# New durations in a planner's table, a margin for attention on TensorE, and later weight sums

## The chip, the cores and the metric

The kernel runs on one core of one Trainium2 chip. The metric is the device time of the whole program in microseconds (us). TensorE is called PE here, its weight loads PEld, VectorE DVE, ScalarE ACT, GpSimd POOL and the queue that issues the DMAs SP.

## The reference, cut to what matters

Everything is fp32. Attention with a sliding window of 64 keys over 4 batches, 8 heads, 576 positions and 64 values a head feeds two feed-forward layers with 2304 tokens:

```
scores = scale * q @ k.T ; masked to 0 <= i - j < 64 ; attn = softmax(scores)
x  = attn @ v                               # (2304, 512)
x  = softplus(x @ w_in) @ w_out             # d_ff 2048, first layer
y  = (sigmoid(x @ w_gate) * (x @ w_val)) @ w_out2   # d_ff 1536, second layer
```

## The kernel before, in words

**Products.** fp32 values are split into a high and a low part, and each product is three matmuls (`mm3`, lines 358 to 360). The weights arrive as fp64 in 512 KB pieces of 128x512 numbers. ACT scales one half of the bits (`w_scale`, line 114), DVE does three bit operations (`w_shift` 119, `w_sign` 123, `w_low` 128), ACT makes the high part (`w_hi`, 134) and POOL the low one (`w_lo`, 139). The 32 pieces of the first layer stay in SBUF.

**First layer.** Tokens go in five blocks (`BLOCKS1`: 512, 384, 384, 512, 512). A slot is one group of 12 matmuls: `m1_proj(b, f)` (h from x and w1) or `m1_out(b, f)` (adds into four accumulators acc). Block b has 16 of each, alternating, so block 0 is slots 0 to 33, and block 1 begins at slot 30. Piece i of the weights is first needed by slot i. Between the two stand `m1_act` (softplus on ACT, 377), `g_hi` (ACT, 384) and `g_lo` (POOL, 390). h has two PSUM buffers, so a projection waits for the softplus of two projections earlier.

**Attention.** 36 groups of 64 queries; the first 8 (`NG0`, "early") come before block 0, the others are done while the block before theirs is in the slots. One group is: `att_scores` (PE, 256), `att_max` (DVE, 268 and 271), `att_exp` (ACT, 283; for later groups in pairs, with a table load before and one after, at the next softplus), `att_sum` (DVE, 288 and 289), `att_norm` (POOL, 294), a transpose (PE 302 in block 0; from groups of block 2 on through DVE 310 and two DMAs, `pd` and `pt`, 316 and 323), `att_values` (PE, 340), `att_hi` (ACT, 348), `att_lo` (DVE, 353, writes xt). Scores, transposes and values share two PSUM buffers named at: values wait until `att_max` or `att_lo` has emptied one.

**Second layer.** Three stages of 768 tokens by a scheme with seven products (x2 blocks and weight sums). The weight sums (here: combos) are made during the first layer, one for each of 12 f: `c_load` of two pieces, scale and bit operations as above, `c_sums` (DVE, 153 to 155), `c_sum4` (160), `c_hi` (ACT, 178), `c_lo` (POOL, 182) and four `c_send` DMAs (187) back to HBM. `wc_load` reads them in the second layer.

**The order.** Every step is given a slot and a rank by hand (`at`). Combo f stands at slot `COMBO0 + int(COMBO * f)`. For all that lies before the second layer (`t < end`, slot 158 or so), `lead_in` then simulates the engines: among the next `AHEAD` steps by rank it takes the one that can start soonest (ties within `SLACK` by rank), with the duration that `traits` gives for it, and emits the instructions in that order. Each engine then runs its own instructions strictly in that order and waits by semaphores. So a duration in the table changes no instruction, only where it stands in its engine's queue. A DMA has in `traits` an issue time and a latency.

Of the kernel before, what the change touches and what calls it, by code (L numbers as in the profile page):

```python
# [19 lines left out]
BLOCKS1 = [512, 384, 384, 512, 512]  # L20
HALF = 384
LAG = 2
LEAD = 7
COMBO0, COMBO = 36, 9.8
WO0, WO = 6, 10
FAR = 2
RG = 0.9
SLACK = 0.15
AHEAD = 160
STB, PB, VB, GB, RB, BB = 3, 2, 2, 3, 3, 3  # L30

# [2 lines left out]
def tile_kernel(ctx: ExitStack, tc: tile.TileContext, qk, vt, w1, w2, wg, wv, wo, out):  # L34
# [21 lines left out]
    w1, w2, wg, wv, wo = (w.bitcast(U32) for w in (w1, w2, wg, wv, wo))  # L56
# [141 lines left out]
    NG0 = BLOCKS1[0] // Q  # L198
# [331 lines left out]
    for c in range(total2):  # L530
        prods = [(m2_prod, *divmod(c, NF2), k) for k in range(7)]
        outs = [(m2_out, *divmod(c - 1, NF2), i) for i in range(NCH)] if c else tail
        for entry in "M0 M1 o0 o1 M2 M3 o2 M4 M5 o3 o4 M6 o5".split():
            kind, k = (prods, outs)[entry[0] == "o"], int(entry[1])
# [158 lines left out]
    index = {key: i for i, (key, _) in enumerate(allw)}  # L693
    groups = range(NT // Q)

    def turned(g):
        return (att_blocks if grp_block[g][0] >= FAR else att_transpose, g)

    def traits(fn, a, *rest):
        early = fn.__name__.startswith(("att", "v_")) and a < NG0  # L700
        f = rest[-1] if rest else a
        if fn in (w_load, c_load):
            freed = (w_low, a) if fn is w_load else (c_send, (a - NSLOT) // 2, "av"[a % 2])
            f = (a - NSLOT) // 2 - 1
            deps = [(w_load, NSLOT - 1)] if f == -1 else [(c_hi, f, "x")] if f >= 0 else []
# [5 lines left out]
        if fn is att_scores:  # L711
            if early:
                deps = [(k_load, a // 2), (q_load, a)] + [(k_load, a // 2 - 1)] * (a % 2 == 0 and a > 0)
                return "pe", 0.55, 0, deps, [(f"s{a % 2}", 1, (att_max, a))]
            return "pe", 0.45, 0, [(qk_load, a), turned(a - 2)], [("at", 2, (att_max, a))]
        if fn is att_max:
            return "dve", 1.4, 0, [(att_scores, a)], [] if early else [("p", PB, turned(a))]
        if fn is att_exp:
            if early:
                return "act", 1.65, 0, [(att_max, a)], []  # L720
            return "act", 7.2, 0, [(att_max, a - 1), (att_max, a)], []
        if fn is att_sum:
            return "dve", 0.35, 0, [(att_exp, exp_of(a))], []
        if fn is att_norm:
            return "pool", 1.05, 0, [(att_sum, a)], []
        if fn is att_transpose:
            return "pe", 0.5, 0, [(att_norm, a)], [(f"t{a % 2}", 1, (att_copy, a)) if early else
                                                   ("at", 2, (att_copy, a))]
# [6 lines left out]
        if fn is att_copy:  # L735
            return "act", 0.6, 0, [(att_transpose, a)], [("pt", 2, (att_values, a))]
        if fn is att_values:
            return "pe", 0.5, 0, [(att_copy, a), (att_fetch, a), (v_load, a)], [("at", 2, (att_lo, a))]
        if fn is att_hi:
            b, off = grp_block[a]  # L740
            return "act", 0.4, 0, [(att_values, a)], [("xt", 2, (m1_proj, b, NF1 - 1))] * (off == 0)
# [2 lines left out]
        if fn is w_scale:  # L744
            kind, f = allw[a][0]
# [1 line left out]
            order = [(w_scale, NSLOT - 1) if a < NSLOT + 2 else (c_sums, (a - NSLOT) // 2 - 1)] * (a >= NSLOT)  # L747
            return "act", 0.67, 0, [(w_load, a), (c_load, a)] + order, [("bits", BB, freed)]
        if fn is w_shift:
            return "dve", 0.5, 0, [(w_scale, a)], []  # L750
        if fn in (w_sign, w_low):
            return "dve", 0.85, 0, [(w_shift if fn is w_sign else w_sign, a)], []
        if fn is w_hi:
            deps = [(w_low, a)]
            if a < NSLOT:
                deps += [(att_values, g) for g in range(NG0)] * (a >= NSLOT - 2 * NG0)
            else:
                kind, f = seq1[place[a]][0]
                deps.append((m1_proj if kind == "w1" else m1_out, NB1 - 1, f))
            return "act", 0.62, 0, deps, []  # L760
        if fn is w_lo:
            return "pool", 1.4, 0, [(w_hi, a)], []
        if fn is c_sums:
            return "dve", 1.3, 0, [(w_low, index["wg", a]), (w_low, index["wv", a])], [("bits", BB, (c_lo, a, "x"))]
        if fn is c_sum4:
            return "dve", 0.45, 0, [(c_sums, a), (c_lo, a, "a")], []
        if fn is c_hi:
            dep = {"a": (w_low, index["wg", a]), "s4": (c_sum4, a)}.get(f, (c_sums, a))
            return "act", 0.62 if f != "s4" else 0.4, 0, [dep], [("raw", RB, (c_send, a, "x"))] * (f == "x")
        if fn is c_lo:  # L770
            return "pool", 1.3 if f != "s4" else 0.75, 0, [(c_hi, a, f)], []
        if fn is c_send:
            return "sp", 1.0, 2.0, [(c_lo, a, f)], []
        if fn is m1_proj:
            deps = [(w_lo, index["w1", f])] + [(att_lo, g) for g in groups if grp_block[g][0] == a]
            deps += [slots[pos[fn, a, f] - 1]] * (a + f > 0)
            return "pe", 12 * (BLOCKS1[a] / 2400 + 0.0137), 0, deps, [(f"h{f % 2}", 1, (m1_act, a, f))]
        if fn is m1_act:
            return "act", 0.56, 0, [(m1_proj, a, f)], [("tb", 2, (g_lo, a, f))]
        if fn is g_hi:  # L780
            return "act", 0.56, 0, [(m1_act, a, f)], [("g", GB, (m1_out, a, f))]
        if fn is g_lo:
            return "pool", 1.25, 0, [(g_hi, a, f)], []
        if fn is m1_out:
            deps = [(g_lo, a, f), (w_lo, index["w2", f]), slots[pos[fn, a, f] - 1]]
            deps += [(m1_copy, a - 1, c) for c in range(KC)] * (f == 0)
# [8 lines left out]
            return "sp", 1.2, 2.0, [(swap_pools, 0)] + [(m1_send, b, c) for b in range(2) for c in range(KC)], []  # L795
        if fn is x2_sum:
            deps = [(x2_load, 0, x) for x in ("b11", "b12", "b22", "b21")]
            return "dve", 0.55, 0, deps + [(x2_sum, 0, k, f) for k in range(rest[0])], []
        if fn is x2_hi:
            kind, wf = seq1[2 * rest[0] + f][0]  # L800
            deps = [(x2_sum, 0, k, f) for k in range(4)] + [(m1_proj if kind == "w1" else m1_out, NB1 - 1, wf)]
            return "act", 0.5, 0, deps, []
        if fn is x2_lo:
            return "pool" if f else "dve", 1.05 if f else 0.5, 0, [(x2_hi, a, *rest)], []
        if fn is swap_pools:
            return "none", 0, 0, [(att_lo, g) for g in groups if g >= NG0], []

# [1 line left out]
    def lead_in():  # L809
        nodes = {}  # L810
        for t in sorted(events):
            if t < end:
                for order, n, fn, args in sorted(events.pop(t), key=lambda e: e[:2]):
                    nodes[fn, *args] = (t + order / 1000, *traits(fn, *args))
        free, seen, d_engine, order, rings = defaultdict(float), {}, {}, [], defaultdict(list)
        todo = sorted(nodes, key=lambda k: nodes[k][0])
        deps_of = {k: [d for d in nodes[k][4] if d in nodes] for k in todo}
        while todo:
            ready = []
            for n, key in enumerate(todo[:AHEAD]):  # L820
                rank, engine, us, lat, _, taken = nodes[key]
                deps = list(deps_of[key])
                for name, bufs, _ in taken:
                    if len(rings[name]) >= bufs:
                        deps.append(rings[name][-bufs])
                if all(d in seen for d in deps):
                    start = max([free[engine]] + [seen[d][engine != d_engine[d]] for d in deps])
                    ready.append((start, rank, n, key))
            soonest = min(r[0] for r in ready)
            start, _, n, key = min((r for r in ready if r[0] < soonest + SLACK), key=lambda r: r[1:])  # L830
            rank, engine, us, lat, _, taken = nodes[key]
            for name, _, freed in taken:
                rings[name].append(freed)
            free[engine] = start + us
            seen[key], d_engine[key] = (start + us, start + us + lat + 0.2), engine
            order.append((start, len(order), key))
            del todo[n]
        return [key for _, _, key in sorted(order)]

    with tc.manual_schedule():  # L840
        nc.scalar.preload_act_table_set("exp_and_others")
        late["apool"] = apool_cm.__enter__()
        consts()
        for fn, *args in lead_in():
            fn(*args)
        for i in sorted(events):
            for _, _, fn, args in sorted(events[i], key=lambda e: e[:2]):
                fn(*args)
# [50 lines left out]
```

## Time and profile before

| | us |
|---|---|
| median of three timed runs | 927.37 (925.10 to 928.02) |
| the profiled execution | 923.96 |
| its span, first to last instruction | 922.2 |

The mean granted TensorE clock is 0.989 of full speed. A timeline row has the start, the duration, engine, line and operation, and in brackets how long the engine was idle before it and what released it. "x16" at its end counts merged instructions. First-layer blocks lie at about 39 to 153 us (block 0), 146 to 226 (1), 226 to 311 (2), 311 to 402 (3) and 402 to 495 (4); the second layer follows.

### The profile page before, as it was taken

To read this page: it belongs to the slowest core of one execution; us is meant where nothing else is said; L and a number is where in the kernel's file an instruction comes from. 1 tells how busy PE (TensorE), PEld (TensorE's weight loads), DVE (VectorE), ACT (ScalarE), POOL (GpSimd) and SP (SyncE) were. 2 spreads that over 40 slices of the span, in tenths; PEclk is the share of its full clock that TensorE was granted. 3 is DMA by queue.
4 is the path that set the end of the run, shared out by engine and by line. 5 is a ranking of instruction groups with operands and counts; after the bars stand their busy time and mean duration, and the time that the engine had idled before them with its cause. 6 is when DMAs were issued, how large, how long until landed. Compare 5 with 4: busy or idle time off the path is not lost.

```text
span 922.2 us, 13713 instructions
## 1 busy us (share of the span) xinstructions
PE 892.3 (97%) x5024; PEld 804.5 (87%) x5024; DVE 509.2 (55%) x842; ACT 406.6 (44%) x930; POOL 358.7 (39%) x312
## 2 busy tenths in 40 slices
PE   7799898999989999999999999999999999999998
PEld 7687688999989988888888999998999998999996
DVE  4899997335343645437801667656445446444443
ACT  5787666563755665634522333324222224222222
POOL 2485676342642544445831233325111115111111
PEclk9799999999999999999999999999999999999999
DMA  8546654666666675676404676545564445544441
GB/s 310 188 162 207 208 166 159 220 216 226 216 209 214 226 263 160 200 275 235 159 1 149 228 274 228 205 160 194 194 228 160 160 160 194 195 160 160 160 160 69
DMA packets 56643, 176.54 MB, mean 191 GB/s; under 512 B 6144, under 2 KB 21248, under 8 KB 51968
## 3 DMA queue, kind: packets, MB, share of 16 engines
q1 hardware_dynamic: 56576, 175.66, 54.7%
q8 instruction: 40, 0.66, 0.3%
q14 instruction: 27, 0.22, 0.1%
HBM read 138.67 MB, written 36.96 MB: 190 GB/s over the span
## 4 chain that ended last, share of the span: by engine, by line
PE 79%; DVE 8%; ACT 5%; DMA 4%; issue 3%; POOL 1%; SPq 1%; ACTq 0%; DVEq 0%; POOLq 0%
PE h L358 14%; PE h L359 14%; PE h L360 14%; PE acc L358 9%; PE acc L359 9%; PE acc L360 9%; DMA pd<-pd 2%; DVE bits L123 2%; PE at L256 2%; DVE bits L119 2%; PE at L360 2%; PE at L359 2%; PE at L358 2%; PE acc L256 1%; DVE bits L128 1%
## 5 line engine op out<-in xcount | busy, mean ns | idle before, releaser
L466 DVE TENSOR_TENSOR t<-h,t 128x384 f32<-128x384 f32 x216 | 117.0, 555 | 198.7 <-PE h L360 190.9
L472 POOL TENSOR_TENSOR g<-t,g 128x384 fp32r<-128x384 f32 x72 | 74.9, 1040 | 288.5 <-ACT g L471 278.3
L359 PE MATMUL h<-xc,wc 128*128 128x384 f32 x504 | 169.7, 337 | 0.0
L358 PE MATMUL h<-xc,wc 128*128 128x384 f32 x504 | 169.0, 335 | 0.6 <-DVE t L466 0.4
L360 PE MATMUL h<-xc,wc 128*128 128x384 f32 x504 | 169.2, 336 | 0.0
L390 POOL TENSOR_TENSOR g<-tb,g 128x512 fp32r<-128x512 f32 (+1 forms) x80 | 101.5, 1270 | 139.4 <-ACT g L384 104.2
L358 PE MATMUL h<-xt,w 128*128 128x512 f32 (+1 forms) x320 | 120.4, 376 | 1.2 <-ACT tb L377 1.2
L358 PE MATMUL acc<-g,w 128*128 128x512 f32 (+1 forms) x320 | 121.2, 379 | 0.0
L359 PE MATMUL h<-xt,w 128*128 128x512 f32 (+1 forms) x320 | 118.8, 371 | 0.0
L360 PE MATMUL h<-xt,w 128*128 128x512 f32 (+1 forms) x320 | 118.8, 371 | 0.0
L360 PE MATMUL acc<-g,w 128*128 128x512 f32 (+1 forms) x320 | 118.3, 370 | 0.0
L359 PE MATMUL acc<-g,w 128*128 128x512 f32 (+1 forms) x320 | 118.2, 369 | 0.0
L471 ACT CAST g<-t 128x384 fp32r<-128x384 f32 x72 | 37.0, 513 | 154.8 <-DVE t L466 137.8
L358 PEld LDWEIGHTS h<-xc,wc 128*128 128x128 f32 x504 | 94.6, 188 | 9.0 <-ACT t L478 1.0
L359 PEld LDWEIGHTS h<-xc,wc 128*128 128x128 f32 x504 | 94.5, 188 | 6.5
L360 PEld LDWEIGHTS h<-xc,wc 128*128 128x128 f32 x504 | 94.7, 188 | 0.0
L139 POOL TENSOR_TENSOR w<-bits,w 128x512 fp32r<-128x512 f32 x44 | 63.8, 1450 | 54.4 <-ACT w L134 42.7
L377 ACT ACTIVATE tb<-h 128x512 f32<-128x512 f32 (+1 forms) x80 | 44.1, 551 | 89.0 <-PE h L360 88.8
L128 DVE SCALAR_TENSOR_TENSOR bits<-raw,bits 128x512 uint32<-128x512 uint32 x68 | 73.1, 1075 | 1.8
L358 PEld LDWEIGHTS h<-xt,w 128*128 128x128 f32 x320 | 61.0, 190 | 9.4 <-ACT tb L377 1.5
L358 PEld LDWEIGHTS acc<-g,w 128*128 128x128 f32 x320 | 60.6, 189 | 8.3 <-ACT x L408 0.4
L360 PEld LDWEIGHTS h<-xt,w 128*128 128x128 f32 x320 | 60.8, 190 | 7.9
(93 smaller groups left out, 1542.4 us busy)
## 6 DMA issues: line engine op xcount, KB each, us to landing
wc<-wcd SPq DMA_DIRECT2D x36, 1792.0 KB, 7.3
raw<-in_w SPq DMA_DIRECT2D x32, 512.0 KB, 3.6
qk<-in_qk SPq DMA_DIRECT2D x28, 512.0 KB, 4.8
wcd<-raw SPq DMA_DIRECT2D x24, 512.0 KB, 4.6
v<-in_vt SPq DMA_DIRECT2D x25, 256.0 KB, 4.7
raw<-in_wg SPq DMA_DIRECT2D x12, 512.0 KB, 4.6
raw<-in_wv SPq DMA_DIRECT2D x12, 512.0 KB, 4.5
wcd<-sumr SPq DMA_DIRECT2D x12, 512.0 KB, 5.3
```

The source lines that it names most:

```text
L119: nc.vector.tensor_scalar(out=t, in0=t, scalar1=3, scalar2=None, op0=ALU.logical_shift_left)
L128: nc.vector.scalar_tensor_tensor(out=t, in0=r[:, :, 0], scalar=29, in1=t, op0=ALU.logical_shift_right, op1=ALU.bitwise_or)
L139: nc.gpsimd.tensor_tensor(out=w[:, 1, :], in0=t, in1=w[:, 0, :].bitcast(F32), op=ALU.subtract)
L256: nc.tensor.matmul(out=s[:, j, at0:at0 + n], lhsT=t[:, 0, j, :], rhs=keys[:, j, :n], start=True, stop=True)
L358: nc.tensor.matmul(out=o, lhsT=lh, rhs=rh, start=first, stop=False)
L359: nc.tensor.matmul(out=o, lhsT=lh, rhs=rl, start=False, stop=False)
L360: nc.tensor.matmul(out=o, lhsT=ll, rhs=rh, start=False, stop=last)
L377: nc.scalar.activation(out=t, in_=h_t.pop((b, f)), func=AF.Softplus)
L390: nc.gpsimd.tensor_tensor(out=g[:, 1, :n], in0=t, in1=g[:, 0, :n].bitcast(F32), op=ALU.subtract)
L466: nc.vector.tensor_tensor(out=out, in0=a, in1=b, op=op)
L471: nc.scalar.copy(out=g[:, 0, :HALF], in_=t)
L472: nc.gpsimd.tensor_tensor(out=g[:, 1, :HALF], in0=t, in1=g[:, 0, :HALF].bitcast(F32), op=ALU.subtract)
```

## The change

It changes numbers only: where the combos stand, the durations in `traits`, and a margin in `lead_in`. `ROOM` is added to the time at which a step's inputs are there, for PE steps other than `m1_proj` and `m1_out` whose group is not one of the first 8. No instruction is added or removed. Where only a number changes, the old and the new one are shown with an arrow.

```diff
-COMBO0, COMBO = 36, 9.8
+COMBO0, COMBO = 52, 8.4
+ROOM = 0.5
 att_scores:
-            return "pe", 0.45, 0, [(qk_load, a), turned(a - 2)], [("at", 2, (att_max, a))]
+            return "pe", 0.9, 0, [(qk_load, a), turned(a - 2)], [("at", 2, (att_max, a))]
 att_exp (a pair):
-            return "act", 7.2, 0, [(att_max, a - 1), (att_max, a)], []
+            return "act", 5.9, 0, [(att_max, a - 1), (att_max, a)], []
 att_norm:       "pool", 1.05 -> 1.09        att_values:  "pe", 0.5 -> 0.62
 w_shift:
-            return "dve", 0.5, 0, [(w_scale, a)], []
+            return "dve", 0.74, 0, [(w_scale, a)], []
 w_sign, w_low:
-            return "dve", 0.85, 0, [(w_shift if fn is w_sign else w_sign, a)], []
+            return "dve", 0.9 if fn is w_sign else 1.15, 0, [(w_shift if fn is w_sign else w_sign, a)], []
 w_lo:           "pool", 1.4 -> 1.49         c_sums:      "dve", 1.3 -> 1.7
 c_sum4:         "dve", 0.45 -> 0.55         c_lo:        "pool", 1.3 -> 1.37 (s4 stays 0.75)
 m1_act:
-            return "act", 0.56, 0, [(m1_proj, a, f)], [("tb", 2, (g_lo, a, f))]
+            return "act", BLOCKS1[a] / 1000 + 0.09, 0, [(m1_proj, a, f)], [("tb", 2, (g_lo, a, f))]
 g_hi:           "act", 0.56 -> BLOCKS1[a] / 1000 + 0.11
 g_lo:           "pool", 1.25 -> BLOCKS1[a] * 0.0028
 x2_sum:         "dve", 0.55 -> 1.2          x2_lo:       "pool" 1.05 -> 1.37, "dve" 0.5 -> 1.1
 lead_in:
-                    start = max([free[engine]] + [seen[d][engine != d_engine[d]] for d in deps])
+                    room = ROOM if engine == "pe" and key[0] not in (m1_proj, m1_out) and key[1] >= NG0 else 0
+                    start = max([free[engine]] + [seen[d][engine != d_engine[d]] + room for d in deps])
```

## Rows read from the trace of the kernel before

**Rows 1.** Page: span, then busy time of each engine (share, instructions).

```profile
span 922.2 us, 13713 instructions
PE 892.3 (97%) x5024; PEld 804.5 (87%) x5024; DVE 509.2 (55%) x842; ACT 406.6 (44%) x930; POOL 358.7 (39%) x312
```

**Rows 2.** Windows: length, each engine's busy us (instructions), granted clock, DMA share, GB/s.

```profile
0.00:100.00 100.00, 87.32 (x558) 74.86 (x559) 83.08 (x120) 69.88 (x183) 58.24 (x52) 0.93 0.63 213
100.00:200.00 100.00, 94.20 (x601) 85.04 (x600) 68.22 (x104) 66.25 (x156) 55.99 (x47) 0.98 0.57 184
200.00:300.00 100.00, 93.76 (x650) 91.85 (x649) 41.09 (x85) 55.04 (x140) 40.52 (x40) 0.98 0.69 225
...
400.00:500.00 100.00, 100.00 (x443) 82.86 (x444) 45.52 (x53) 38.99 (x74) 52.05 (x38) 1.00 0.45 162
...
110.00:120.00 10.00, 10.00 (x44) 8.05 (x40) 8.63 (x16) 9.89 (x26) 4.69 (x4) 0.83 0.67 233
270.00:280.00 10.00, 9.81 (x63) 9.78 (x64) 2.53 (x5) 2.20 (x5) 5.39 (x6) 0.83 0.69 215
```

**Rows 3.** Waits of PE, 0 to 310 us: total us, times, longest.

```profile
PE at L340 <- DVE xt L353: 8.5, 6, 3.2
PE at L340 <- DVE p L268: 5.3, 2, 3.4
...
PE at L256 <- DVE xt L353: 2.4, 1, 2.4
PE at L340 <- DMA pt<-pd: 2.1, 3, 1.2
PE h L358 <- ACT tb L377: 1.2, 1, 1.2
```

**Rows 4.** Timeline of PE: the two waits for `att_max` in block 0.

```profile
79.82 0.68 PE L340 MATMUL at<-pt,v 64*64 64x64 f32 x16 [1.94 <-DVE p L268]
...
109.52 0.69 PE L340 MATMUL at<-pt,v 128*64 128x64 f32 x16 [3.40 <-DVE p L268]
```

**Rows 5.** Groups on DVE by form, 40 to 150 us: busy us, mean ns.

```profile
L128 DVE SCALAR_TENSOR_TENSOR bits<-raw,bits 128x512 uint32<-128x512 uint32 x30 | 39.7, 1323 | 0.9
L123 DVE SCALAR_TENSOR_TENSOR bits<-raw,bits 128x512 uint32<-128x512 uint32 x30 | 28.6, 953 | 1.0
L119 DVE TENSOR_SCALAR bits<-bits 128x512 uint32<-128x512 uint32 x29 | 23.9, 825 | 2.8 <-ACT bits L114 2.8
```

**Rows 6.** Timeline of DVE ahead of the longest wait.

```profile
106.04 0.41 DVE L119 TENSOR_SCALAR bits<-bits 128x512 uint32<-128x512 uint32 x1
...
107.22 1.65 DVE L128 SCALAR_TENSOR_TENSOR bits<-raw,bits 128x512 uint32<-128x512 uint32 x1
108.79 0.68 DVE L268 SCALAR_TENSOR_TENSOR p<-at,mask 128x512 f32<-128x512 f32 x1
```

**Rows 7.** Timeline: pieces 16 and 28 finished on POOL, their slots begun on PE.

```profile
91.05 1.47 POOL L139 TENSOR_TENSOR w<-bits,w 128x512 fp32r<-128x512 f32 x1
133.79 1.49 POOL L139 TENSOR_TENSOR w<-bits,w 128x512 fp32r<-128x512 f32 x1 [1.28 <-ACT w L134]
...
92.72 0.48 PE L358 MATMUL h<-xt,w 128*128 128x512 f32 x1
136.82 0.39 PE L358 MATMUL h<-xt,w 128*128 128x512 f32 x1
```

**Rows 8.** Timeline of ACT around a pair of exponentials in block 2.

```profile
226.26 0.66 ACT L114 ACTIVATE bits<-raw 128x512 f32<-128x512 f32 x1 [4.45 <-DMA raw<-in_wv]
227.87 1.28 ACT L283 ACT_TABLE_LOAD   x1
232.37 1.28 ACT L377 ACT_TABLE_LOAD   x1
```

**Rows 9.** Combos: line 155, one for each (ns min/median/max, first and last start).

```profile
L155 DVE TENSOR_TENSOR bits<-bits x12: 411/418/419, 150.8 to 452.4; 128x256 f32<-128x256 f32 x12
```

**Rows 10.** Group of line 114 over the span: its idle time and who ended it.

```profile
L114 ACT ACTIVATE bits<-raw 128x512 f32<-128x512 f32 x68 | 45.5, 670 | 41.1 <-DMA raw<-in_wv 22.6 <-DMA raw<-in_wg 11.8 <-DMA raw<-in_wo 3.0
```

More of the change, by code (lines that the diff above doesn't have):

```diff
@@ L724, in traits @@
         if fn is att_norm:
-            return "pool", 1.05, 0, [(att_sum, a)], []
+            return "pool", 1.09, 0, [(att_sum, a)], []
         if fn is att_transpose:
@@ L737, in traits @@
         if fn is att_values:
-            return "pe", 0.5, 0, [(att_copy, a), (att_fetch, a), (v_load, a)], [("at", 2, (att_lo, a))]
+            return "pe", 0.62, 0, [(att_copy, a), (att_fetch, a), (v_load, a)], [("at", 2, (att_lo, a))]
         if fn is att_hi:
@@ L761, in traits @@
         if fn is w_lo:
-            return "pool", 1.4, 0, [(w_hi, a)], []
+            return "pool", 1.49, 0, [(w_hi, a)], []
         if fn is c_sums:
-            return "dve", 1.3, 0, [(w_low, index["wg", a]), (w_low, index["wv", a])], [("bits", BB, (c_lo, a, "x"))]
+            return "dve", 1.7, 0, [(w_low, index["wg", a]), (w_low, index["wv", a])], [("bits", BB, (c_lo, a, "x"))]
         if fn is c_sum4:
-            return "dve", 0.45, 0, [(c_sums, a), (c_lo, a, "a")], []
+            return "dve", 0.55, 0, [(c_sums, a), (c_lo, a, "a")], []
         if fn is c_hi:
@@ L770, in traits @@
         if fn is c_lo:
-            return "pool", 1.3 if f != "s4" else 0.75, 0, [(c_hi, a, f)], []
+            return "pool", 1.37 if f != "s4" else 0.75, 0, [(c_hi, a, f)], []
         if fn is c_send:
@@ L778, in traits @@
         if fn is m1_act:
-            return "act", 0.56, 0, [(m1_proj, a, f)], [("tb", 2, (g_lo, a, f))]
+            return "act", BLOCKS1[a] / 1000 + 0.09, 0, [(m1_proj, a, f)], [("tb", 2, (g_lo, a, f))]
         if fn is g_hi:
-            return "act", 0.56, 0, [(m1_act, a, f)], [("g", GB, (m1_out, a, f))]
+            return "act", BLOCKS1[a] / 1000 + 0.11, 0, [(m1_act, a, f)], [("g", GB, (m1_out, a, f))]
         if fn is g_lo:
-            return "pool", 1.25, 0, [(g_hi, a, f)], []
+            return "pool", BLOCKS1[a] * 0.0028, 0, [(g_hi, a, f)], []
         if fn is m1_out:
@@ L797, in traits @@
             deps = [(x2_load, 0, x) for x in ("b11", "b12", "b22", "b21")]
-            return "dve", 0.55, 0, deps + [(x2_sum, 0, k, f) for k in range(rest[0])], []
+            return "dve", 1.2, 0, deps + [(x2_sum, 0, k, f) for k in range(rest[0])], []
         if fn is x2_hi:
@@ L803, in traits @@
         if fn is x2_lo:
-            return "pool" if f else "dve", 1.05 if f else 0.5, 0, [(x2_hi, a, *rest)], []
+            return "pool" if f else "dve", 1.37 if f else 1.1, 0, [(x2_hi, a, *rest)], []
         if fn is swap_pools:
```

## The prediction, on record before the change was built

> **What bounds the kernel now.** I read the page's line of busy times first, then the windows, then PE's waits, and then the timeline of the engines around each wait. PE is busy for 892.3 of 922.2 us [rows 1], so at most 29.9 us are idle, and everything else that reordering could give back is time at the lower clock. The windows [rows 2] say where: from 400 to 500 us PE is busy for all of 100.00 us, while the first three windows lose 12.7, 5.8 and 6.2 us. The change acts on the first layer and on what leads into the second; the second layer's own order is written by hand and stays. So the question is what happens to the waits before 311 us.
>
> Those are few [rows 3]. Early attention (before 39 us) waits for xt: of the 8.5 us in that row one wait of 3.2 us belongs to block 2, and 5.3 us are early. Block 0 has 5.3 us for `att_max` (p, line 268) and 2.4 us for xt at scores, 7.7 us together. Blocks 1 and 2 have 3.2 us for xt, 2.1 us for the DMA'd pt, and 1.2 us for a softplus, 6.5 us together. Two of the waits cost more than themselves. In the windows from 110 and from 270 us the granted clock is 0.83 [rows 2]: PE had stood idle for 3.40 us just before the first [rows 4] and for 3.2 us around 270, and then ran part of the window at 1.2 instead of 2.4 GHz. A mean of 0.83 over 10 us is 1.7 us of work lost, each time. Block 0 thus offers 7.7 + 1.7 = 9.4 us, blocks 1 and 2 offer 6.5 + 1.7 = 8.2 us, the early part 5.3 us.
>
> **Why block 0 waits.** The reader is to compare the table with the trace. The planner gave the three bit operations 0.5 + 0.85 + 0.85 = 2.2 us a piece; between 40 and 150 us they took 0.825 + 0.953 + 1.323 = 3.10 us [rows 5]. Over 30 pieces DVE falls 27 us behind its plan, as far as the semaphores let it. The rows ahead of the longest wait show it [rows 6]: `att_max` starts at 108.79, right behind the bit operations of line 128, and PE, whose order has values next, stands until 109.52. Planned honestly, either `att_max` comes earlier on DVE or values later on PE.
>
> The same rows show why the planner can't win all of it. One and the same operation takes 0.41 us in one place and 0.825 us in the mean of block 0 [rows 5, 6] (line 119), and DVE is filled with these operations, which feed PE too. Piece 16 leaves POOL at 91.05 + 1.47 = 92.52 us and its slot begins at 92.72, with 0.2 us to spare; piece 28 leaves at 135.28 and its slot begins at 136.82, with 1.5 us to spare [rows 7]. If PE doesn't stand at 77 and at 106 us, the slots come sooner and the pieces don't.
>
> **The change part by part**, against the profiled execution's 923.96 us (922.2 us of span and 1.8 us around it).
>
> *Durations of the bit operations, `w_lo`, `c_sums` and the other DVE and POOL rows.* The new table gives 0.74 + 0.9 + 1.15 = 2.79 us a piece, 0.31 us short of block 0's 3.10 [rows 5], so the lag falls from 27 to 9 us over 30 pieces. I expect the waits for `att_max` and xt to shrink. What is late next are the pieces: with their times unchanged, PE can come forward by 0.2 us before slot 16, by 1.5 us before slot 28 [rows 7], and by 1.5 + 2.4 = 3.9 us once the third wait has gone too. Bounds: 0 gained (every attention step drawn ahead on DVE pushes the pieces back by its own 0.68 us and more) and 9.4 us. I take 3.0 us, near the cap of 3.9 that the rows give, less one `att_max` of 0.68 us [rows 6] put ahead of a piece.
>
> *`ROOM`, and the longer scores and values.* Affected are the PE steps of 28 groups. A wait that stays in the same place shrinks by up to 0.5 us. The three pt waits sum to 2.1 us with a longest of 1.2 [rows 3]; taking the other two as 0.9 together, they lose 0.5 + 0.7 = 1.2 us. The xt wait of 3.2 us loses 0.5. The softplus wait is a projection's and gets no margin. Behind a postponed attention step its group's ACT and DVE steps come later; PE has slots to run meanwhile, and if at some point it hasn't, the cost is 0.5 us for that step. Together 1.7 us gained, between 0 and the 8.2 us of blocks 1 and 2.
>
> *`att_exp` from 7.2 to 5.9 us.* From the table load at 227.87 to the end of the next table load at 232.37 + 1.28 = 233.65 ACT is held for 5.8 us of which 1.28 us are the second load [rows 8]. So 5.9 us is right for the pair with both loads, and the old 7.2 was 1.4 us too long. What stood behind the exponentials was planned late and is now planned up to 1.3 us sooner. Cost nothing, hidden by `ROOM` for 0.5 us of it; if that cover fails, 0.8 us for a pair. Bounds -0.8 and +0.8 us for a pair, and I take 0.
>
> *`m1_act`, `g_hi`, `g_lo`, x2.* A few hundredths up or down in the first two, and x2 steps that run after 400 us, where PE is busy without a gap [rows 2]. Nothing; if that cover is gone, one x2 step of 1.2 us.
>
> *Combos later.* Combo 0 moves from slot 36 to 52, combo 11 from 143 to 144. Each moves 2 scales on ACT, 6 bit operations and 4 sums on DVE, 4 `c_hi` and 4 `c_lo`, and on SP 2 loads and 4 sends. Until now line 155 ran from 150.8 to 452.4 us [rows 9], close to the slots written down, so I expect the first one some 40 us later and the last where it was. Block 1 then has two combos in place of three, block 2 three as before, block 3 four in place of three. What a combo costs is seen on ACT, not on DVE: its scale stands at the head of ACT's queue until the load has landed, 22.6 + 11.8 = 34.4 us over 24 scales, 1.4 us each [rows 10], and whatever ACT should do next waits too. The softplus wait of 1.2 us is such a case: a scale held ACT for 4.45 us until 226.26, and the exponentials followed [rows 8]. On SP the sends now pass loads of q, k and v of other groups. Last comes the end: the last combo's slot moves by one, and it stands 43 us ahead of the second layer (452.4 against 495). Bounds: 1.2 us gained, or one more wait like block 2's of 3.2 us with its 1.7 us at the lower clock. Nearest is the row of no change, since block 2 keeps its three; I take 0.
>
> *Early part.* `ROOM` leaves it out, and only the order on DVE can move. Bounds: 5.3 us gained, or 3.1 us lost, if a whole piece of bit operations [rows 5] comes ahead of the last `att_lo`. I take 0.
>
> Sum: 3.0 + 1.7 = 4.7 us gained. 923.96 - 4.7 = 919.3 us. The profiled execution lay 3.4 us below the median of the timed runs, 927.37; on that, 922.7 us.
>
> **A page's rule against the trace.** Line 119 takes 0.41 us in one place and 0.825 us on average in block 0, where POOL works beside it [rows 5, 6]. The Trainium skill's page "SBUF — State Buffer" ("SBUF: two separate sides") says that DVE instructions with two SBUF inputs or in a two-port mode and GpSimd instructions share one pair of ports under an exclusive lock, held for the whole instruction. The trace agrees in kind. By that rule DVE and POOL are one resource in block 0, the pieces could come no sooner in any order, and the block would give 0 of its 9.4 us; that is the first rival below.
>
> **The rivals.**
> 1. *The pieces take over.* The waits for `att_max` go and waits for `w_lo` at slots 12 to 28 come in their place: block 0 gives the 0.2 us of slot 16 and, the idle time being cut into smaller pieces, half of its 1.7 us of clock; later blocks give some 0.5. 0.2 + 0.8 + 0.5 = 1.5, so 925.9 us. For it: 0.2 us of slack [rows 7]. Against: 2.4 us of block 0's waits lie behind slot 28. The page named above would have it so.
> 2. *Slower: ACT blocks at worse places in blocks 2 and 3.* The new order lets scales of combos wait for their loads just ahead of a pair of exponentials. One of block 2's three combos now ends in 3.2 + 1.7 = 4.9 us; if two of the seven combos of blocks 2 and 3 more do so, that is +9.8 us, less the 4.7 us above: 927.4 + 5.1 = 932.5 us. It decides where a scale's wait and the 5.8 us of a pair [rows 8] together exceed the time until PE needs the next h or at buffer. For it: block 2's slots are the short ones, and DMA shares there are 0.69 [rows 2]. Against: block 3's slots are a third longer, and its attention waited for next to nothing.
> 3. *Everything settles.* All waits for attention go, block 0 gives its 3.9 us and 1.7 us of clock, and blocks 1 and 2 give 6.4 of their 8.2 us: 12.0 us, so 915.4 us. For it: the table's largest error, DVE's, is mostly mended. Against: the DMA steps' issue times in the table stay as they were.
> 4. *The change doesn't do what it says:* combos follow data and not slots, and come as early as before. That part stands at 0 in the sum, so this moves no time, and has no chance apart from the others.
>
> **How the numbers follow.** Forecast 0.42 (own range 919 to 924.5), rival 1 0.28, rival 2 0.17, rival 3 0.13. A measurement of this kernel tells about 0.3%, 2.8 us, from no change: below 924.6 is faster, above 930.2 slower. Faster: 0.42 + 0.13 = 0.55; same 0.28; slower 0.17. The range takes rival 3 at its time, and rival 2 up to about half: 914 to 931 us.
>
> **What would show it.** Right: `att_max` no longer ends waits of 2 us or more on PE in block 0; no window with the clock at 0.83 near 110 us; the pieces' slack at slot 16 to 28 near nothing; pt waits under 1 us; the first line 155 near 200 us. Wrong: PE waits for `w_lo` in sum as long as before (rival 1); new waits of 3 us for xt or a softplus after 226 us (rival 2); a gain of more than 4 us in block 0, which would mean that the pieces came sooner; a second layer that starts with a gap.

## The result, and the profile after

The changed kernel takes 936.98 us (median of 7 runs, 932.88 to 940.10) against 925.52 us for the kernel before on the same chip (924.85 to 929.49): a ratio of 1.0113, interval 1.0081 to 1.0145. It is slower by some 10.5 us. The profiled execution took 933.5 us, with this head of the page and these windows (columns as in [rows 1, 2]; PE, DVE, ACT and POOL run as many instructions as before):

```profile
span 931.7 us, 13725 instructions
PE 897.0 (96%) x5024; PEld 807.3 (87%) x5024; DVE 514.5 (55%) x842; ACT 405.7 (44%) x930; POOL 358.7 (38%) x312
```

```profile
100.00:200.00 100.00, 95.82 (x607) 86.66 (x606) 69.81 (x102) 64.09 (x153) 57.25 (x46) 0.97 0.58 197
200.00:300.00 100.00, 92.57 (x634) 90.34 (x633) 43.18 (x84) 53.85 (x139) 39.17 (x38) 0.95 0.66 216
...
110.00:120.00 10.00, 9.52 (x56) 7.70 (x57) 9.20 (x17) 9.21 (x27) 4.76 (x4) 0.66 0.86 295
...
270.00:280.00 10.00, 6.90 (x40) 6.81 (x41) 2.51 (x9) 5.44 (x12) 6.46 (x6) 0.66 0.69 211
300.00:310.00 10.00, 5.62 (x45) 5.20 (x44) 6.92 (x10) 3.72 (x9) 5.03 (x4) 0.92 0.43 137
310.00:320.00 10.00, 9.97 (x59) 9.88 (x60) 2.67 (x8) 6.96 (x22) 4.24 (x4) 0.74 0.68 220
```

The stretch from 270 to 320 us is new: PE stands idle for 3.1 and 4.4 us of two windows, and runs at a granted clock of 0.66 and 0.74 in or after them. PE's waits from 0 to 311 us, to be held against [rows 3] (line numbers are one higher), say what PE waited for:

```profile
PE at L341 <- DMA pt<-pd: 11.4, 3, 5.0
PE at L341 <- DVE p L269: 5.5, 4, 2.4
...
PE at L341 <- DVE xt L354: 3.9, 5, 1.4
PE at L257 <- DVE xt L354: 1.2, 1, 1.2
```

The waits for xt fell, those for `att_max` (p) stayed, and the wait for the transposed attention that comes through two DMAs rose from 2.1 to 11.4 us. Its three places, in PE's timeline:

```profile
216.33 1.12 PE L341 MATMUL at<-pt,v 128*64 128x64 f32 x16 [2.12 <-DMA pt<-pd]
...
273.10 1.12 PE L341 MATMUL at<-pt,v 128*64 128x64 f32 x16 [4.99 <-DMA pt<-pd]
...
310.03 1.12 PE L341 MATMUL at<-pt,v 64*64 64x64 f32 x16 [4.34 <-DMA pt<-pd]
```

Equal work in both timelines says when the time is lost. The first projection begins at 38.96 before and 36.32 after (2.6 us sooner), block 1 at 145.85 and 144.76, a projection of block 2 at 240.19 and 241.29, the first projection of block 3 at 311.33 and 320.21 (first row before, second after):

```profile
311.33 0.39 PE L358 MATMUL h<-xt,w 128*128 128x512 f32 x1
```

```profile
320.21 0.39 PE L359 MATMUL h<-xt,w 128*128 128x512 f32 x1
```

So 7.8 of the 9.5 us arise between 241 and 320 us, at the last two waits. The later one has most of it: a projection of block 2 that stands between the two begins at 284.67 before and at 288.04 after, so 2.3 us are lost at the wait at 273 (where the kernel before stood for xt, 3.2 us) and 5.5 us at the one at 310. From there both kernels keep their distance (the second layer begins at 495.49 and 504.51).

SP's queue shows what made pt late. Its rows are DMA issues, with start and duration of the issue; first the kernel before, then the one after, ahead of the wait at 273:

```profile
246.76 0.85 SPq L187 DMA_DIRECT2D wcd<-raw  x2
247.70 0.73 SPq L187 DMA_DIRECT2D wcd<-sumr  x1
249.60 0.33 SPq L107 DMA_DIRECT2D raw<-in_wg  x1
250.03 1.36 SPq L187 DMA_DIRECT2D wcd<-bits  x1
251.55 0.74 SPq L107 DMA_DIRECT2D raw<-in_wv  x1
252.38 0.97 SPq L224 DMA_DIRECT2D v<-in_vt  x2
253.40 0.49 SPq L316 DMA_DIRECT2D pd<-pd  x1
```

```profile
244.56 0.43 SPq L188 DMA_DIRECT2D wcd<-raw  x1
248.87 0.35 SPq L108 DMA_DIRECT2D raw<-in_wg  x1
249.32 0.38 SPq L188 DMA_DIRECT2D wcd<-raw  x1
254.75 0.33 SPq L108 DMA_DIRECT2D raw<-in_wv  x1
255.17 0.38 SPq L188 DMA_DIRECT2D wcd<-sumr  x1
255.65 0.38 SPq L188 DMA_DIRECT2D wcd<-bits  x1
256.12 1.22 SPq L225 DMA_DIRECT2D v<-in_vt  x1
257.44 0.89 SPq L317 DMA_DIRECT2D pd<-pd  x1
```

A combo's load writes a `raw` tile that one of the last combo's sends must have left. Before, both sends from `raw` go out together, and both loads follow. After, each load stands directly behind the send that it waits for, and nothing behind it can issue: SP stands from 244.99 to 248.87 and from 249.70 to 254.75, and the attention's pd is issued at 257.44 in place of 253.40. Its data had been there since 249.86, when DVE's transpose ended. SP's own waits from 240 to 262 us (before, then after) and that transpose:

```profile
SPq L107 <- DMA wcd<-raw: 1.1, 1, 1.1
```

```profile
SPq L108 <- DMA wcd<-raw: 8.8, 2, 5.0
```

```profile
249.15 0.71 DVE L311 STREAM_TRANSPOSE pd<-p 128x512 f32<-128x512 f32 x1 [2.11 <-POOL p L295]
```

The issue rows of the loads are 0.33 to 0.35 us long; the wait is the gap ahead of them. The two sends landed at 248.86 and 254.73 by the trace, and the loads are recorded from 248.87 and 254.75. The Trainium skill ("Perfetto Trace Analysis", DMA Instruction — HWDGE) says that on trn2 the issuing sequencer does the semaphore wait, and the profiled window begins after it. The trace agrees.

### The profile page after: what moved, and what is told of

Read it like the earlier page. It is cut to its first block, busy times and chain, and to the rows that moved or that the text cites. A ratio compares the mean times of both kernels' runs of the same rounds, so it can differ in the third digit from the quotient of the medians.

```text
span 931.7 us, 13725 instructions
## 1 busy us (share of the span) xinstructions
PE 897.0 (96%) x5024; PEld 807.3 (87%) x5024; DVE 514.5 (55%) x842; ACT 405.7 (44%) x930; POOL 358.7 (38%) x312
## 4 chain that ended last, share of the span: by engine, by line
PE 72%; DVE 9%; DMA 9%; ACT 4%; issue 3%; SPq 1%; POOL 0%; ACTq 0%; POOLq 0%; DVEq 0%
PE h L359 13%; PE h L360 13%; PE h L361 13%; PE acc L359 8%; PE acc L360 8%; PE acc L361 8%; DVE bits L124 3%; DMA pd<-pd 3%; DVE bits L120 2%; DMA wcd<-raw 2%; PE at L257 2%; DVE bits L129 2%; PE at L361 2%; PE at L360 2%; DMA raw<-in_wv 2%
## 5 line engine op out<-in xcount | busy, mean ns | idle before, releaser
L391 POOL TENSOR_TENSOR g<-tb,g 128x512 fp32r<-128x512 f32 (+1 forms) x80 | 103.7, 1298 | 145.9 <-ACT g L385 119.0
L359 PE MATMUL acc<-g,w 128*128 128x512 f32 (+1 forms) x320 | 123.2, 385 | 0.1
L360 PE MATMUL acc<-g,w 128*128 128x512 f32 (+1 forms) x320 | 120.3, 376 | 0.0
L361 PE MATMUL acc<-g,w 128*128 128x512 f32 (+1 forms) x320 | 120.1, 375 | 0.0
L359 PEld LDWEIGHTS acc<-g,w 128*128 128x128 f32 x320 | 62.1, 194 | 8.8 <-DVE x L411 0.5
L361 PEld LDWEIGHTS acc<-g,w 128*128 128x128 f32 x320 | 62.0, 194 | 7.8
L360 PEld LDWEIGHTS acc<-g,w 128*128 128x128 f32 x320 | 62.2, 195 | 7.2
```

Source lines behind the costliest of these rows:

```text
L359: nc.tensor.matmul(out=o, lhsT=lh, rhs=rh, start=first, stop=False)
L360: nc.tensor.matmul(out=o, lhsT=lh, rhs=rl, start=False, stop=False)
L361: nc.tensor.matmul(out=o, lhsT=ll, rhs=rh, start=False, stop=last)
L391: nc.gpsimd.tensor_tensor(out=g[:, 1, :n], in0=t, in1=g[:, 0, :n].bitcast(F32), op=ALU.subtract)
```

## The experiments

Theories: **Q** (queue): a load that waits for a landing send holds SP, and pd behind it; the order of loads, sends and pd on SP decides. **T** (table): the new durations place attention worse by themselves. **M** (margin): `ROOM` delays attention until its data are late. **P** (pieces, the first rival of the prediction): block 0 is bound by the supply of weights. Ratios are to the kernel before on the same chip, with 95% intervals.

**The parts, alone and in pairs.** Each kernel has only the named hunks of the diff.

> The kernel before with the new durations alone (no margin on PE, combos where they were). The theory that the durations make the loss (they shift the order on SP, so that pd and pt transfers go out late, while their own DMA entries stay too short): 6 to 12 us slower than before, with pt waits on PE of 8 us or more in sum before 320 us (the changed kernel has 11.4). The rival that the later combos make it: within 3 us of before, pt waits near 2 us. If two parts are needed together: within 3 us as well.

> The kernel before with the margin of 0.5 us for attention steps on PE alone. The theory that the durations make the loss: within 3 us of before, or up to 2 us faster, since a wait that stays in place can only shrink; pt waits below 2.1 us. The rival that any new order deals the waits anew: a change of more than 4 us either way, with waits at other places than before.

> The kernel before with the combos written 16 slots later alone. In the changed kernel the first five combos came within 4 us of where they were before and only the later ones 10 to 20 us later, so by the theory that the durations make the loss this is within 3 us of before. The rival that the later combos put their loads ahead of pd and pt on SP: 5 us or more slower, pt waits of 8 us or more after 260 us.

> The changed kernel with the old durations (margin and later combos stay). The theory that the durations make the loss: back to within 3 us of before, pt waits at most 3 us in sum. The rival that the combos or the margin make it: still 6 us or more slower than before, pt waits of 8 us or more.

> The changed kernel with the combos where they were. Theory of the queue: the loss is gone, 923 to 927 us, pt waits at most 4 us in sum, and block 0 shows waits for the low parts of the weights in place of some for att_max. Theory that durations and margin together carry it: 931 us or more, with the three pt waits of the changed kernel.

> The new durations and the later combos, without the margin: the one pair of the three parts not yet run. If the margin has no part in the loss (the durations and the combos' spacing make it between them), this takes the changed kernel's time, 934 to 938 us, with both pt waits of 4 us or more in block 2. If the loss needs all three parts, it takes 928 to 931 us like the combos alone and like margin and combos. Its plan has the first load of combo 4 ahead of two sends of combo 3, so one pt wait of 4 us or more between 265 and 280 us is expected by either.

| durations | ROOM | combos 52, 8.4 | us | ratio | pt waits, 40 us to the end of block 2 |
|---|---|---|---|---|---|
| x | | | 926.2 | 1.0002 [0.9978, 1.0027] | 5.3 |
| | x | | 926.3 | 1.0000 [0.9976, 1.0025] | 2.9 |
| | | x | 930.0 | 1.0032 [1.0009, 1.0054] | 6.0 |
| x | x | | 925.2 | 0.9995 [0.9975, 1.0015] | 4.5 |
| | x | x | 929.8 | 1.0043 [1.0019, 1.0068] | 7.4 |
| x | | x | 937.0 | 1.0119 [1.0096, 1.0141] | 12.6 |
| x | x | x | 937.0 | 1.0113 [1.0081, 1.0145] | 11.4 |

The margin neither costs nor gives (M falls). The durations alone cost nothing (T falls as a cause by itself), the combos 0.3%, the two together 1.2%: 0.85% of 925 us, some 8 us, belongs to their meeting. Several expectations missed in part. The combos alone cost 3.0 us with 6.0 us of pt waits, at the edge of the one theory and short of the other's 5 and 8. Without the durations the kernel is 4 us slower, between the two bounds given. With durations and margin the pt waits are 4.5 and not at most 4 us, and block 0 shows no waits for low parts. With durations and combos the time came as forecast, but of the two long pt waits one is 7.6 us and the other 3.2. The waits of the margin alone from 40 to 153 us bear on P:

```profile
PE h L361 <- POOL w L140: 3.1, 2, 1.5
...
PE at L341 <- DVE p L269: 2.1, 3, 0.9
```

With the margin the waits for `att_max` fall from 5.3 to 2.1 us and waits for `w_lo`, which the kernel before hardly has there, take 3.1 us in their place. In the changed kernel this exchange does not come: it has 5.5 us for `att_max` and no row for `w_lo`.

**The order on SP.** First the spacing without the later start, and a later start without the spacing; then the changed kernel with the loads' ranks two slots later, which puts them behind the sends of the combo before.

```diff
-COMBO0, COMBO = 36, 9.8
+COMBO0, COMBO = 36, 8.4     # spacing_alone
+COMBO0, COMBO = 41, 9.8     # start_alone
-            at(t - 2 + k, -60, c_load, i + k)
+            at(t + k, -60, c_load, i + k)     # loads_behind, on the changed kernel
```

> The kernel before with the combos closer together alone (start at slot 36 as before, 8.4 slots apart in place of 9.8). Theory of the spacing: 8.4 slots put combo 4's first load (raw from wg) ahead of combo 3's second send on SP, each load waits there for a send to land, and the pd and pt transfers of block 2 queue behind: a pt wait of 4 us or more near 273 us, 3 to 5 us slower than before, as with the later combos alone (+3.5). Theory that it is the later start: the same as before within 2 us, pt wait there under 2 us.

> The kernel before with the combos five slots later alone (slot 41, still 9.8 apart; no later start fits in front of the second layer at that distance). Theory of the spacing: combo 3's two sends stay together ahead of combo 4's load, so within 2 us of before and pt waits at most 3 us in sum. Theory of the later start: a third of the 16 slots, so 1 us or more slower, with a pt wait near 273 us that has grown.

> The changed kernel with the rank of the combos' loads two slots later, so that they come behind combo 3's sends in SP's queue again; all else as in the changed kernel. Theory of the queue: the pt wait of 5.0 us near 273 us falls below 2.5 us and with it the low clock there (3.4 us), 5 to 8 us faster than the changed kernel, so 929 to 932 us. Theory that the durations or the margin carry the loss: within 2 us of the changed kernel's 937.

Measured: spacing alone 945.73 us, 1.0226 [1.0204, 1.0249]; start alone 922.23 us, 0.9974 [0.9958, 0.9990]; loads behind 930.56 us, 1.0064 [1.0045, 1.0082]. The spacing costs 20.9 us, far more than the 3 to 5 expected, and not under the label that was expected. Its waits on PE, 40 to 400 us, and SP in the same kernel:

```profile
...
PE h L358 <- ACT xt L348: 4.8, 1, 4.8
PE at L340 <- DVE bits L119: 3.7, 1, 3.7
PE at L340 <- DVE pd L310: 3.6, 1, 3.6
```

```profile
242.30 0.38 SPq L107 DMA_DIRECT2D raw<-in_wg  x1
242.77 0.38 SPq L187 DMA_DIRECT2D wcd<-raw  x1
251.21 0.33 SPq L107 DMA_DIRECT2D raw<-in_wv  x1
251.59 0.42 SPq L187 DMA_DIRECT2D wcd<-sumr  x1
252.06 2.89 SPq L323 DMA_DIRECT2D pt<-pd  x4
```

Here one load holds SP from 243.15 to 251.21, 8.1 us, with the pt loads behind it; values begin at 258.08, after a wait that is put down to a bit operation. Values read pt and v and no bits: the bit operation only happened to end at 257.96. The pt loads, issued from 252.06 on, landed by 257.72, so the late loads are what values waited for. This hold is not the 20.9 us, though. By equal work it costs 4.5 us, which the kernel before loses too by 277 us; some 18 us come between 285 and 330 us, where loads hold SP again and PE waits for pt and for xt (4.8 us). Which hold costs what there was not traced, and the same spacing from slot 52 on costs 3.0 us. With the loads behind the sends SP has both sends from `raw` at 245.51, the loads at 249.77 and 251.00, pd at 253.25, and the first wait is 2.49 in place of 4.99 us. By the ratios this gives back 0.49%, 4.5 us, though the two intervals just touch; by equal work in the two traces 2.9 us come back at this wait. Q holds for the first wait; the second stays at 3.59 us.

**Longer DMA times in the table.** If the planner puts loads badly because it believes a send to land 2.0 us after its issue, measured times should help. The issue times and latencies of four kinds of DMA were set from the trace, on the changed kernel, on the same with combos at 41 and 9.8, and on start_alone.

```diff
 att_send: -"sp", 0.5, 2.0   +"sp", 0.5, 4.0      att_fetch: -"sp", 0.6, 2.5   +"sp", 1.75, 1.8
 c_send:   -"sp", 1.0, 2.0   +"sp", 1.0, 3.4      c_load:    -"sp", 1.6, 2.0   +"sp", 1.6, 2.8
```

> The changed kernel with longer DMA times in the planner's table, from issue to landing as the trace has them (pd 4.7, pt 3.8, sends and loads of combos 4.6 us), no step's rank touched. Theory that the loss is attention on PE planned against DMA times that are too short, behind loads that stand waiting on SP: the pt waits of 11.4 us fall to 4 us or less and the kernel takes 924 to 930 us. Theory that the ranks of loads and sends are the whole cause: combo 4's load still ahead of combo 3's second send, so 933 us or more.

> The same with the combos at slot 41, 9.8 apart: everything that helped, together (durations, margin, start, DMA times). By the theory of the queue pt waits of 2 us or less in sum and 917 to 922 us. If the gains are those of single orders and don't add up: 922 to 928 us.

> The kernel before with the combos at slot 41, 9.8 apart, and the longer DMA times, without the new durations and the margin. Theory of the queue: the pt wait of 3.9 us that the run with the start alone still has falls below 1 us, 918 to 921 us. If the longer times only deal a new order: 921 to 927 us.

Measured 931.30 (1.0068 [1.0046, 1.0090]), 934.78 (1.0096 [1.0073, 1.0119]) and 932.74 us (1.0068 [1.0046, 1.0089]). All three miss. The first is 0.45% faster than the changed kernel, with 9.6 us of pt waits left where 4 or less were expected (the two intervals overlap a little); the third is 10 us slower than the same kernel without the new times (922.23). A table closer to the trace is no better plan by itself.

**The second wait.** On loads_behind, a wait in the planner alone for one load (the second of combo 6, then that of combo 5), and then for one group's values:

```diff
+            deps += [(att_send, 28)] * (a == 45)     # load_after_pair
+            deps += [(att_send, 26)] * (a == 43)     # load_after_fetch
-            return "pe", 0.62, 0, [(att_copy, a), (att_fetch, a), (v_load, a)], [("at", 2, (att_lo, a))]
+            return "pe", 0.62, 0, [(att_copy, a), (att_fetch, a), (v_load, a)] + [(m1_out, 2, 12)] * (a == 27), [("at", 2, (att_lo, a))]     # values_apart
```

> The combos' loads behind the sends, as in the run before of that kind, and besides the second load of the combo whose load held SP until 290.04 there is put behind the pd send of the pair that PE then waited for. Queue theory: with the load out of its way pd goes out some 3 us sooner, the pt wait of 3.59 us near 306 falls below 1.5 us, and the time falls by 3 to 5 us from 930.6 to some 926. Rival (the second wait is one for the transposes and DMAs of the pair itself, 5 to 7 us each, in series; the load is not what ends last): pd goes out sooner and the wait stays at 3 us or more, the time within 1.5 us of 930.6. Second rival: the postponed scale stands at the head of ACT's queue and a softplus or xt wait of 2 us or more comes up in block 3; the time stays or rises.

> The combos' loads behind the sends (930.6 us in its run), and one load more put back: that of combo 5's second piece, which in that run went out at 290.04, having held SP from 287.7, and ahead of a pd send whose data DVE had transposed by 284.70 and which went out at 291.52. It now stands behind that pair's pt loads. Nothing else on SP changes place. Queue theory: pd goes out some 2 to 3 us sooner, the pt wait near 306 falls from 3.59 us to 1 us or less, and the time falls by 2 to 4 us to 926 to 929. Rival (the pair's own two DMAs under a full DMA load, 6.4 us for pd alone, make the wait): pd sooner, the wait 3 us or more, the time 930 to 932. Second rival: the scale of that piece, which stood 6.52 us at the head of ACT's queue, stands there longer still, and PE waits for a softplus (tb): time 930 or above with a wait of 2 us or more for ACT.

> The combos' loads behind the sends (930.6 us), and the values of the second group of the pair that makes the wait of 3.59 us near 306 put behind one more group of 12 products, as the kernel before has them (there the two groups' values begin at 301.73 and 304.66 with a group of products between; with the new durations they stand back to back). Theory: the two groups' transposed attention comes through one pd tile and so in series, pt loads 6 us apart, and the new durations ask for the second one slot too early; the wait falls to 1 us or less and the time by 2.5 to 4 us, to 926.5 to 928. Rival (the later pd is the whole cause, and the place of the values none): PE meets another wait of 2 us or more within the next slots and the time stays within 1.5 us of 930.6.

The first, 931.53 us, 1.0055 [1.0023, 1.0087], moved the wrong load: the load that held SP belongs to the combo before and still goes out ahead of pd, at 290.75. The second moved the right one: SP goes from the sends to pd without a stop, and yet the wait is 4.96 us and the time 932.23 us, 1.0038 [1.0018, 1.0058]. SP there:

```profile
294.52 0.91 SPq L317 DMA_DIRECT2D pd<-pd  x1
300.52 1.74 SPq L324 DMA_DIRECT2D pt<-pd  x4
302.31 0.43 SPq L108 DMA_DIRECT2D raw<-in_wv  x1
302.84 0.38 SPq L242 DMA_DIRECT2D qk<-in_qk  x1
303.32 0.38 SPq L317 DMA_DIRECT2D pd<-pd  x1
308.30 0.80 SPq L324 DMA_DIRECT2D pt<-pd  x2
```

The two groups of a pair go through one pd tile, one behind the other: the first's send lands after 6.0 us, only then DVE transposes the second (300.56), whose send takes 5.0 us more. The second group's pt is issued 7.8 us behind the first's here, and 6.0 to 6.1 us in the changed kernel and in loads_behind, where a 512 KB load of qk stands ahead of the second pd as well; before, without it, 3.6 us. What remains is when PE asks for it. Before, a group of products stands between the values of the two:

```profile
301.73 0.69 PE L340 MATMUL at<-pt,v 128*64 128x64 f32 x16 [0.20 <-DMA pt<-pd]
304.66 0.68 PE L340 MATMUL at<-pt,v 64*64 64x64 f32 x16
```

In the plans of the changed kernel and of loads_behind none does. The third kernel puts it back:

```profile
304.17 0.69 PE L341 MATMUL at<-pt,v 128*64 128x64 f32 x16 [0.99 <-DMA pt<-pd]
...
309.20 0.68 PE L341 MATMUL at<-pt,v 64*64 64x64 f32 x16 [1.15 <-DVE p L269]
```

927.51 us, 1.0027 [1.0005, 1.0050], pt waits 2.1 us in place of 6.1 up to 311 us, near what its theory expected (1.15 us are left in that place). Back-to-back values are the durations' doing: they are there with the durations alone too (wait in that place 1.39 us), and dear only once the combos make pd late. With the combos alone the place costs next to nothing (that kernel is 6.2 us behind the one before ahead of it and 6.6 us after it), in the changed kernel 5.5 us. That is the meeting of the two parts. In values_apart itself pt is still issued 6.0 us behind the first's; only the asking is later. Against loads_behind this is 0.37%, 3.4 us; the two intervals still touch, so the size is less sure than the place. What is left, 0.27%, I have not traced.

**Block 0's supply.** The margin alone, without `w_sign` on the 32 pieces of the first layer; the weights' signs are left out of what is computed.

```diff
-        nc.vector.scalar_tensor_tensor(out=t, in0=r[:, :, 1], scalar=0x80000000, ...)
+        if i >= len(seq1):
+            nc.vector.scalar_tensor_tensor(out=t, in0=r[:, :, 1], scalar=0x80000000, ...)
```

> The kernel with the margin alone, without the sign operation (line 123 of the kernel before, 0.95 us a piece on DVE in block 0) on the 32 pieces of the first layer; their weights lose their signs. If the supply of pieces bounds block 0: the waits for low parts (1.5 us at 93 and at 122 us) go and most of those for att_max and xt with them, and block 0 ends 4 us or more earlier. If attention's own chain bounds it: the waits for the low parts go, those for att_max and xt stay within 1 us, and block 0 ends 1.5 to 3 us earlier.

913.42 us, 0.9868 [0.9849, 0.9888]. In the window from 40 to 150 us PE is busy throughout at the full clock, where the kernel before has 102.26 at 0.98 (same columns; first before, then this one):

```profile
40.00:150.00 110.00, 102.26 (x556) 84.41 (x555) 104.41 (x124) 79.18 (x171) 75.34 (x52) 0.98 0.57 191
```

```profile
40.00:150.00 110.00, 110.00 (x627) 93.71 (x626) 80.09 (x106) 84.61 (x186) 79.92 (x60) 1.00 0.59 200
```

DVE's share falls from 0.95 to 0.73, and all waits of block 0 of 0.5 us or more go: from the first projection to block 1 it takes 96.0 us in place of 106.9. P holds in part: what bounds block 0 is DVE's work on the pieces, and the orders tried here only share out that bound. Whether PE then lacks a piece or an attention step that stood behind one on DVE, this run does not separate, since it frees both.

**A faster version.** The margin with the start at 41, and the same with three loads of block 2 behind the pd send that they went ahead of:

```diff
+            deps += [(att_send, 22)] * (a in (40, 41)) + [(att_send, 26)] * (a == 43)
```

> The kernel before with the first combo at slot 41 (spacing 9.8) and with the margin. The former alone took 922.2 us, the margin alone 926.3 against 926.5. If parts add up: 921 to 923 us, with the waits for att_max in block 0 at 2 us in sum in place of some 4. If what a part is worth hangs on where the loads and the pd sends meet in block 2 (the queue theory, and what the sums of parts have shown so far), any time from 920 to 930 us, and its pt waits tell which: below 922 with less than 2 us of them, above 926 with more than 5.

> The best so far (first combo at slot 41, spacing 9.8, margin; 921.5 us), with three loads of combos in block 2 put behind the pair's pd send that they went ahead of: both of combo 4, and the second of combo 5. Its two pt waits were 3.16 us at 267.57 and 1.46 us at 300.78, behind pd sends that took 6.5 and 7.5 us to their pt loads with 512 KB loads just ahead of them. Queue theory: both waits fall below 1 us and the time to 917 to 920 us. Rival (combos made later hand the wait on, as every sum of parts before): 921 to 926 us with a new wait for tb, xt or pt of 2 us or more after 250 us.

921.53 us, 0.9959 [0.9939, 0.9979], as if its two parts added up, and 920.44 us, 0.9934 [0.9908, 0.9960]. Both beat both kernels. The moved loads shorten the longest pt wait from 3.16 to 2.06 us, not below 1, and raise the clock from 220 to 311 us to 1.00; against start_and_margin alone the gain is inside the intervals.

## Why the prediction was wrong

*The early part and block 0.* Taken: 0 and 3.0 us gained. Measured: 2.6 us gained before the first projection (inside its bound of 5.3), and 1.5 us lost from there to block 1. The waits for `att_max` stay at 5.5 against 5.3 us, with the longest 2.39 in place of 3.40 us [rows 3, 4], and the window from 110 us has 0.66 in place of 0.83 [rows 2]. The expected sign ("no longer ends waits of 2 us or more", "no 0.83 near 110") fails. The step "I expect the waits for `att_max` and xt to shrink" fails for `att_max`; xt at scores falls from 2.4 to 1.2 us. The cap by the pieces was the right thought, and its size too kind: margin_alone swaps one wait for the other at no gain, as the first rival had it, and margin_no_sign frees what no order did.

What the account of block 0 did not see is why a bit operation takes 0.69 us here and 1.65 us there. In the kernel before, the operation of line 128 in [rows 6] starts at 107.22, inside this operation on POOL, and takes 1.65 us; with POOL idle it takes 0.68 us:

```profile
106.85 1.47 POOL L139 TENSOR_TENSOR w<-bits,w 128x512 fp32r<-128x512 f32 x1 [1.28 <-ACT w L134]
...
112.50 0.68 DVE L128 SCALAR_TENSOR_TENSOR bits<-raw,bits 128x512 uint32<-128x512 uint32 x1
```

It is so without exception from 40 to 150 us: 45 of the 88 bit operations that start there do so while POOL is in an operation, and each of them ends 0.28 us (line 119) or 0.55 us (lines 123 and 128) after POOL's does; the other 43 take 0.41 to 0.42 or 0.68 to 0.69 us. `att_max` at 108.79 takes its usual 0.68 us, though POOL is in an operation from 108.46 to 110.00. The page that stood beside the first rival, the Trainium skill's "SBUF — State Buffer" ("SBUF: two separate sides"), lets a DVE instruction with two SBUF inputs or in a two-port mode and a GpSimd one block each other fully for a whole instruction. The trace agrees for lines 123 and 128, which read two inputs from SBUF; in which mode line 119 runs, with one input, no row shows.

So the recorded durations hold the waiting: of the 92.2 us of bit operations in [rows 5], some 39 are waits for POOL. The 3.10 us a piece are no property of the operations but of the order they stand in, and a table of fixed durations can't have them right. The mean of POOL's `w_lo` stays at 1489 ns without `w_sign` (1494 before), since it is mostly DVE that does the waiting.

*ROOM.* Taken: 1.7 us gained in blocks 1 and 2. Measured alone: 1.0000. The pt waits of blocks 1 and 2 did not shrink (2.9 against 2.1 us), and the xt wait of 3.2 us lost some 0.3.

*Combos later.* This is the step that failed: "Nearest is the row of no change ... I take 0", bounded by one wait of 4.9 us. Alone the later combos cost 3.0 us, still inside that bound; with the durations they cost some 11. Two things were wrong in the step. The combos do not move as written: line 156 starts for the first five at 151.2, 188.4, 212.5, 231.5 and 269.7 us (before: 150.8, 186.1, 212.5, 230.4, 266.1), for the planner takes a step when its data and engine are free; the last comes 9.9 us later. The page's row of after, against [rows 9]:

```profile
L156 DVE TENSOR_TENSOR bits<-bits x12: 411/418/1511, 151.2 to 462.3; 128x256 f32<-128x256 f32 x12
```

So rival 4 was true of the first five, but "this moves no time" was not: the spacing changed which load met which send. Second, the price was looked for on ACT, where a scale waits for its load [rows 10], and the working passed over SP in one sentence without a price ("sends now pass loads of q, k and v"). The load's own wait for a landing send, 8.8 us of SP's time from 240 to 262 us, and pd and pt behind it, was never costed; the gap ahead of line 107 in SP's timeline of before, 1.1 us, would have shown that there is such a wait. The second rival had the right blocks, the right sign and a time (932.5 us) within 5 of the measured, but that is luck, for its mechanism was another one: no softplus or xt wait of 3 us came up in block 2.

*Durations, and the sum.* Taken as harmless outside DVE. They are harmless alone; the longer table pushed two groups' values together, which is the second wait, 5.5 of the 7.8 us. Parts were summed one by one, and 8 of the 10.5 us lie in two parts together: in an order made by a planner the sum of parts is no forecast.

## What to carry to other kernels

Before a step with DMAs is moved, read the one queue that issues them: which transfer there waits for a semaphore, for how long, and what stands behind it. A transfer that waits for another's landing should not be queued ahead of anything urgent. Before a measured mean goes into a planner's table, look whether it holds waits for another engine. And price edits of a planner's input as one order, since their effects don't add.

## What the runs showed of the hardware that was not expected

- A 512 KB send lands after 2.6 to 8.9 us: in the median over the changed kernel 4.3 us from `raw` and 5.3 us from `sumr`, 8.9 us for `sumr` at 285 us in loads_behind, with DMA near 400 GB/s. A load waiting for one cost SP up to 8.1 us. pd, 256 KB, takes 5.2 to 7.2 us when it is issued between 291 and 297 us (before, changed, loads_behind, load_after_fetch).
- A bit operation on DVE that starts inside an operation of POOL lasts until 0.28 or 0.55 us after its end, and holds that wait in its recorded duration (0.69 us becomes 1.65 us).
- A wait's label can name an operation that has nothing to do with it and only ended at the same time: with the spacing alone 7.3 us stand under DVE's bits and pd, which ended some 0.1 us before PE went on; the last pt loads had landed 0.36 and 0.14 us before.
- Waits of 4 to 5 us on PE came with granted clocks of 0.66 to 0.74 in windows that hold them or follow; one of 2.39 us with 0.66, one of 2.12 us with 0.83, and one of 3.40 us before the change with 0.83.
- Kernels with the same order up to there waited 1.9, 4.2, 1.9 and 4.75 us for one softplus near 208 us (loads_behind, load_after_fetch, load_after_pair, values_apart). The order of instructions does not fix it, and it may be why these kernels scatter by 5 us.
